# A greedy instruction list for attention: other durations, other due times, and another order for the first two units

## The chip, the cores and the metric

The kernel runs on one core of one Trainium2 chip. The metric is the device time of one execution in microseconds (us); lower is better. Before the change it is 993.29 us, the median of three runs (992.11 to 995.47).

## The reference, cut to what matters

Three stages follow each other: attention with rotary positions, an ELU network, and a bilinear network.

```python
# attention: batch 4, heads 8, sequence 576, head size 64
q_rot, k_rot = rotate(q), rotate(k)              # x1*cos - x2*sin, x1*sin + x2*cos
scores = (1 / sqrt(64)) * q_rot @ k_rot.T
attn = exp(scores - max(scores)); attn = attn / sum(attn)
x = (attn @ v)                                   # to 2304 tokens x 512
h = x @ w_in                                     # 512 x 2048
g = where(h > 0, h, exp(min(h, 0)) - 1)
x = g @ w_out                                    # 2048 x 512
return (((x @ w1) * (x @ w2)) @ w3) @ w_out2
```

## The kernel before, in words

**Units and chunks.** Attention works on 16 units, each two heads of one batch. A unit's 576 query rows are cut in four chunks of 128 rows (c = 0 to 3, both heads) and a last one of 64 rows of each head (c = 4). For c = 0 to 3 TensorE runs three parts: `Pa` (score products of the first head's first half), `Pb` (the rest of the first head and half of the second) and `Pc` (the rest), with transposes of an earlier chunk between the products. c = 4 is `S4` (`scores_4`); its stationary operand is `diag`, a block-diagonal copy of the last 64 query columns. Between these stand, for the unit before, `T4`, `l1`, `r1`, `s0` (small transposes) and `PV` (weights times v, L583 and L589).

**What each chunk costs the other engines.** VectorE takes the negative row maximum of the scores (`most`, L465), ScalarE the exp (`expo_s`, L471). TensorE needs that exp twice: to transpose it (L416) and because the exp frees the score bank in PSUM that the next chunk writes. Evacuations of the transposes (L478 on ScalarE, L480 on VectorE) go to either engine.

**Rope.** Each unit's q (576 columns) and k (640 columns) are turned by five steps each: two products with the tables `tab` (L329), an add (L332), a copy of the high part (L81, always ScalarE) and the low part (L338). The steps other than the copy go to GpSimd or VectorE. `tab[:, 1]` is the table, `tab[:, 0]` the same times the score scale. Unit 0 is turned by `first_rope` on VectorE (L358, L362, L372) in pieces, ahead of the list; its last 320 q columns come in the list (`first`, L358 to L374). Unit 1 is turned by `part` in the list: k on GpSimd, q on VectorE. GpSimd then makes unit 0's diagonal (L85) and the scaled table (L740).

**Weights.** During attention 16 tiles of the 64-bit w_in and w_out are turned into float32 (`weight_steps`): one step on ScalarE (L123), three on VectorE (L126, L129, L132).

**The list.** Nothing of this is ordered by hand. `Plan.add` takes an operation with its engine (or a choice, "pool/dve"), its duration `busy`, its latency `late` to others, a due time and its dependencies; `Plan.order` then plays the program through and emits, engine by engine, the operation that can start first, ties (within `AHEAD`, 0.2 us on VectorE) broken by due time. `ready` (not before) is at least the due time less `HOLD_0` (12 us). For a choice, `RATHER` adds a handicap: VectorE 1.2 us for rope, ScalarE 0.3 us beside GpSimd. Operations marked `lock`, and all on GpSimd, exclude each other in the list between GpSimd and VectorE. Due times come from `nom`, a clock that starts at `AT_0` and adds `busy * UNIT / 14.7` for every TensorE part:

```python
def PE(key, busy, fn, *deps, late=0.2):
    nom[key] = clock[0]
    clock[0] += busy * UNIT / 14.7
    plan.add(key, "pe", busy, late, 0.0, fn, *deps)
```

The list fixes only the order on each engine. On the chip each engine runs its queue in order and waits by semaphores for data; GpSimd's rope steps and VectorE's weight steps share no data and so no semaphore. SP issues all loads in order. `warm_up` (L826) puts dummy products on TensorE at the beginning (30, and a few between the first chunks).

Of the kernel before, what the change touches and what calls it, by code (L numbers as in the profile page):

```python
# [12 lines left out]
ALU = mybir.AluOpType  # L13
# [14 lines left out]
UNIT = 16.0  # L28
AT_0 = 14.0
# [29 lines left out]
def kernel(  # L59
# [156 lines left out]
    class Plan:  # L216
# [10 lines left out]
        def order(self):  # L227
# [51 lines left out]
    with ExitStack() as c1:  # L279
# [328 lines left out]

        def last_t(i, name):
# [8 lines left out]
        for i in range(NU + 1):  # L618
            for c in range(5):
# [34 lines left out]
                if c == 3 and more:
                    PE(("s0", i), 0.5, lambda i=i: small_0(i), ("spread", i, 0), *last_t(i, "s0"))
                if c == 3 and j >= 0:
                    PE(("PV", j, 1, 1), 1.0, lambda j=j: weigh(j, 1, (4,)), ("evl", j, 1))
                if c == 4 and j >= 0:
                    PE(("PV", j, 1, 2), 1.1, lambda j=j: weigh(j, 1, (2, 3)))

        MX, EX = OP("dve", 0.68, 0.16), OP("act", 0.73, 0.12)
        EV = OP("dve/act", dict(dve=0.58, act=0.51), 0.18)
        SP_ = lambda key, kb, due, fn, *deps, ready=EARLY: plan.add(key, "sp", 0.5, kb / 280.0, due, fn, *deps, ready=ready)
        end = clock[0]
        for i in range(NU):
# [22 lines left out]
            OP("dve/act", dict(dve=0.75, act=0.68))(("evl", i, 1), t + 0.8, lambda e, i=i: evacuate_tails(i, 1, e), ("l1", i), ("PV", i - 1, 1, 1))  # L688
            t = nom["r1", i] + 0.5
            OP("dve/act", dict(dve=0.36, act=0.29))(("evr", i, 1), t + 1.5, lambda e, i=i: evacuate_spread(i, 1, e), ("r1", i))  # L690
            t = nom["s0", i] + 0.5
            OP("dve/act", dict(dve=0.36, act=0.29))(("evl", i, 0), t + 0.4, lambda e, i=i: evacuate_tails(i, 0, e), ("s0", i), ("PV", i - 1, 0, 1))
            OP("dve/act", dict(dve=0.34, act=0.27))(("evr", i, 0), t + 0.8, lambda e, i=i: evacuate_spread(i, 0, e), ("s0", i), ("evl", i, 0))
            for hf in range(2):
# [3 lines left out]
                OP("pool/act", (dict(pool=0.4, act=0.35), dict(pool=0.9, act=0.75))[hf])(("spread", i, hf), t - (1.2, 2.0)[hf], lambda e, i=i, hf=hf: spread(i, hf, e), ("norm", i, hf), (("s0", "r1")[hf], i - 1))  # L698
# [4 lines left out]
                OP("dve", 0.36 + 0.04 * hf)(("wd", i, hf), t + (2.4, 2.2)[hf], lambda i=i, hf=hf: weighed(i, hf), dep, ("evr", i, hf))  # L703
# [17 lines left out]
        for k_ in range(5):  # L721
            eng = ("dve", "dve", "dve", "act", "dve")[k_]
            OP(eng, (0.4, 0.4, 0.4, 0.37, 0.4)[k_], lock=eng == "dve")(
                ("low", 0, 0) if k_ == 4 else ("first", 0, k_), 17.0 + 0.5 * k_, lambda k_=k_: first_step(0, 0, 256, S, dve, k_),
                *((("first", 0, k_ - 1),) if k_ else ()), ready=16.0,
            )
        OP("pool", 1.1)(("diag", 0), 21.0, lambda: diagonal(u0), ("low", 0, 0))
        for w in (1, 0):
            eng_ = (dve, pool)[w]
            n = (S, SK)[w]  # L730
            for k_ in range(5):
                eng = "act" if k_ == 3 else ("dve", "pool")[w]
                busy = 0.63 if k_ == 3 else (0.68, 1.53)[w]
                OP(eng, busy, lock=eng == "dve")(
                    ("low", 1, w) if k_ == 4 else ("first1", w, k_), (18.0, 12.0)[w] + 1.5 * k_,
                    lambda k_=k_, w=w, n=n, eng_=eng_: first_step(1, w, 0, n, eng_, k_),
                    *((("first1", w, k_ - 1),) if k_ else ()), ready=(17.0, 11.5)[w],
                )
        OP("pool", 0.7)(("diag", 1), 26.0, lambda: diagonal(units[1]), ("low", 1, 0), ("low", 1, 1))
# [818 lines left out]
```

## Time and profile before

| | us |
|---|---|
| median of three runs | 993.29 (992.11 to 995.47) |
| the profiled execution | 992.57 |
| its span (first to last instruction) | 990.8 |
| TensorE busy in it | 959.4 (97%) |
| VectorE, ScalarE, GpSimd busy | 798.4, 656.2, 216.3 |
| attention | from the start to about 289 |

The profile is one execution, recorded by the hardware. Busy shares say how full an engine is, the idle time before an instruction stands in brackets with what ended it. GpSimd has work only in attention.

### The profile page before, as it was taken

How to read it: one execution, taken by the hardware profiler on the slowest of the kernel's cores; microseconds unless marked ns; L12 is line 12 of the kernel's file. 1: busy time of each engine (PE TensorE's matmuls, PEld its weight loads, DVE VectorE, ACT ScalarE, POOL GpSimd, SP SyncE). 2: the span in 40 equal slices, each digit the busy share in tenths (PEclk: the TensorE clock that was granted, in tenths of full speed). 3: DMA queues.
4: the chain of work that ended last, by engine and by line, in shares of the span. 5: the costliest groups of instructions: out<-in, count | busy, mean ns of one | idle time of the engine just before them, and what ended most of it. 6: DMA issues, size and time to landing. Idle time of an engine off the chain costs nothing.

```text
span 990.8 us, 17967 instructions
## 1 busy us (share of the span) xinstructions
PE 959.4 (97%) x6652; PEld 833.1 (84%) x6652; DVE 798.4 (81%) x1488; ACT 656.2 (66%) x1401; POOL 216.3 (22%) x193
## 2 busy tenths in 40 slices
PE   7899989899999999999999999999999999999998
PEld 6666666666679999989999999998899999999997
DVE  7788988889889999999989999856657676675544
ACT  3777867787768778898788877774444354444332
POOL 4887877788620000000000000000000000000000
PEclk8999999999999999999999999999999999999999
DMA  7344443433322455567664676714133242224201
GB/s 242 115 145 132 141 134 121 128 137 116 108 75 80 149 169 157 189 211 233 212 191 132 209 222 228 240 34 153 37 113 88 84 139 85 75 75 153 87 28 64
DMA packets 62535, 134.53 MB, mean 136 GB/s; under 512 B 6640, under 2 KB 15472, under 8 KB 62448
## 3 DMA queue, kind: packets, MB, share of 16 engines
q1 hardware_dynamic: 62448, 133.39, 42.0%
q8 instruction: 52, 0.85, 0.4%
q14 instruction: 35, 0.29, 0.1%
HBM read 107.68 MB, written 25.69 MB: 135 GB/s over the span
## 4 chain that ended last, share of the span: by engine, by line
PE 82%; DVE 10%; ACT 4%; issue 1%; DMA 1%; POOL 1%; SPq 0%; DVEq 0%; ACTq 0%
PE y L929 12%; PE A L1359 10%; PE o L1385 10%; PE A L886 9%; PE B L1359 7%; PE B L886 7%; PE yb L930 6%; PE s L405 6%; PE o L589 5%; PE w L1289 4%; PE ptp L416 3%; DVE nm L465 2%; ACT pr L471 2%; DVE pair L129 1%; DVE pair L126 1%
## 5 line engine op out<-in xcount | busy, mean ns | idle before, releaser
L929 PE MATMUL y<-g,wo 128*128 128x512 f32 x576 | 204.2, 392 | 0.0
L930 PE MATMUL yb<-g,wo 128*128 128x256 f32 x576 | 161.3, 280 | 0.0
L140 DVE TENSOR_TENSOR set<-set 128x512 fp32r<-128x512 f32 (+1 forms) x160 | 98.3, 620 | 41.2 <-ACT set L137 41.1
L405 PEld LDWEIGHTS s<-hl 64*128 64x128 f32 x768 | 88.6, 189 | 50.0 <-ACT pr L471 37.5
L405 PE MATMUL s<-hl 64*128 64x288 f32 x768 | 110.0, 319 | 17.4 <-ACT pr L471 15.8
L929 PEld LDWEIGHTS y<-g,wo 128*128 128x128 f32 x576 | 107.8, 187 | 20.5
L471 ACT ACTIVATE pr<-s,nm 128x576 f32<-128x576 f32 x144 | 105.5, 739 | 22.5 <-DVE nm L465 21.9
L1359 PE MATMUL A<-xc,set 128*128 128x384 f32 x576 | 116.1, 336 | 0.2
L886 PE MATMUL A<-xf,set 128*128 128x384 f32 x552 | 111.5, 337 | 0.8 <-ACT p L943 0.7
L465 DVE TENSOR_REDUCE nm<-s 128x1 f32<-128x576 f32 x144 | 102.8, 748 | 11.6 <-PE s L405 10.8
L1385 PE MATMUL o<-W,g 128*128 128x512 f32 x432 | 111.1, 393 | 0.0
L1359 PEld LDWEIGHTS A<-xc,set 128*128 128x128 f32 x576 | 102.4, 188 | 7.8 <-DVE p L1446 1.0
L930 PEld LDWEIGHTS yb<-g,wo 128*128 128x128 f32 x576 | 108.6, 189 | 0.2 <-ACT xT L939 0.2
L886 PEld LDWEIGHTS A<-xf,set 128*128 128x128 f32 x552 | 93.6, 188 | 4.5 <-ACT p L943 1.5
L81 ACT ACTIVATE g<-p 128x384 fp32r<-128x384 f32 x48 | 25.2, 526 | 107.8 <-DVE p L1446 71.5
L1385 PEld LDWEIGHTS o<-W,g 128*128 128x128 f32 x432 | 80.0, 188 | 12.7
L137 ACT ACTIVATE set<-set 128x512 fp32r<-128x512 f32 (+1 forms) x160 | 89.3, 567 | 1.9 <-DMA set<-kept 1.7
L416 PE MATMUL ptp<-idt,pr 64*128 64x64 f32 x1024 | 87.9, 228 | 0.0
L329 POOL TENSOR_TENSOR raw_qk<-raw_qk,tab 128x640 f32<-128x640 f32 (+1 forms) x56 | 85.7, 1536 | 4.1 <-DMA raw_qk<-k_ 3.7
L1359 PE MATMUL B<-xc,set 128*128 128x384 f32 x432 | 86.5, 334 | 0.0
L886 PE MATMUL B<-xf,set 128*128 128x384 f32 x420 | 84.3, 336 | 0.0
L416 PEld LDWEIGHTS ptp<-idt,pr 64*128 64x128 f32 x1024 | 78.3, 141 | 0.9 <-issue 0.9
(253 smaller groups left out, 1842.5 us busy)
## 6 DMA issues: line engine op xcount, KB each, us to landing
set<-kept SPq DMA_DIRECT2D x120, 256.0 KB, 2.8
raw<-w_ SPq DMA_DIRECT2D x32, 512.0 KB, 4.1
kept<-wr SPq DMA_DIRECT2D x40, 256.0 KB, 3.2
raw_qk<-k_ SPq DMA_DIRECT2D x15, 640.0 KB, 4.0
raw_qk<-q_ SPq DMA_DIRECT2D x15, 576.0 KB, 4.3
raw<-w_in_ SPq DMA_DIRECT2D x16, 512.0 KB, 4.5
raw<-w_out_ SPq DMA_DIRECT2D x16, 512.0 KB, 4.3
w<-kept SPq DMA_DIRECT2D x24, 256.0 KB, 3.0
```

Of the source, the lines that this page charges most:

```text
L137: act.activation(t[:, 0, :w], t[:, 1, :w].bitcast(F32), ACTF.Copy)
L140: eng.tensor_tensor(t[:, 1, :w], t[:, 1, :w].bitcast(F32), t[:, 0, :w].bitcast(F32), op=ALU.subtract)
L329: eng.tensor_tensor(r[:, z], r[:, z], tab[:, w, z, TAB[w]], op=ALU.mult)
L405: pe.matmul(S_t[i, c, e][:, n, :288], w, hl[h, b, at_:at_ + 288], start=(z == 0), stop=(z == 2))
L416: pe.transpose(pts[i, c, z][:, e, kc], pr[h, at_:at_ + P], idt[h, h])
L465: dve.tensor_reduce(nm_t[i, c, e], S_t[i, c, e][:, :, :288], axis=AX.XY, op=ALU.max, negate=True)
L471: act.activation(pr_t[i, c][:, e].rearrange("p (n i) -> p n i", n=2), S_t.pop((i, c, e))[:, :, :288], ACTF.Exp, bias=nm_t.pop((i, c, e)), ...
L886: pe.matmul(banks[b][:, :HF], set_w(n, k, a, c), x[:, e, c], start=(start and i == 0), stop=i == 5, skip_group_check=True,)
L929: pe.matmul(y_t[p, o], w_, g[:, c, :512], start=s, stop=t, skip_group_check=True)
L930: pe.matmul(yb_t[p, o // 2][:, o % 2], w_, g[:, c, 512:], start=s and o % 2 == 0, stop=t, skip_group_check=True,)
L1359: pe.matmul(ps[:, :HB], w[:, a, c * P:(c + 1) * P], x[:, c, b], start=(start and i == 0), stop=i == 5, skip_group_check=True,)
L1385: pe.matmul(outs[p, o], g[:, a, o % 3 * P:o % 3 * P + P], wW[f][:, c], start=(f == 0 and i == 0), stop=(f == NG - 1 and i == 2),)
```

## The change

It does five things. The durations in attention's list are replaced: TensorE's parts by other figures, and those of VectorE, ScalarE and GpSimd by lines in the number of columns (`V_`, `A_`, `G_`, `E_`). `UNIT` goes from 16.0 to 15.5 and `AT_0` from 14.0 to 12.0. The rule of mutual exclusion lets an operation start 0.02 us before the other engine is done. Unit 0's remaining q columns are due at 12 instead of 17, and unit 0's diagonal at 14 instead of 21. Unit 1 is turned by the same steps as the others, each free to go to GpSimd or VectorE, and they wait for unit 0's diagonal; the scaled table is made by ScalarE, in front of the list.

```diff
-UNIT = 16.0
-AT_0 = 14.0
+UNIT = 15.5
+AT_0 = 12.0
+REST = 12.0
...
-                                t = max(t, free.get("lock", t))
+                                t = max(t, free.get("lock", t) - 0.02)
...
+        V_ = lambda n, fast=False: 0.00052 * n + 0.065 if fast else 0.00104 * n + 0.068
+        A_ = lambda n, sb=True: 0.00104 * n + (0.023 if sb else -0.005)
+        G_ = lambda n, tt=True: 0.00217 * n + 0.15 if tt else 0.000845 * n + 0.155
+        E_ = lambda n: dict(dve=V_(n), act=A_(n, False))
...
-                    PE(("Pa", i, c), 0.5, lambda i=i, c=c, back=back: part_a(i, c, back), *ha, ("low", i, 0), ("low", i, 1), *ta[:2])
-                    PE(("Pb", i, c), 0.4, lambda i=i, c=c: part_b(i, c), *hb)
-                    PE(("Pc", i, c), 0.5, lambda i=i, c=c, back=back: part_c(i, c, back), *ta)
+                    PE(("Pa", i, c), 0.53, lambda i=i, c=c, back=back: part_a(i, c, back), *ha, ("low", i, 0), ("low", i, 1), *ta[:2])
+                    PE(("Pb", i, c), 0.39, lambda i=i, c=c: part_b(i, c), *hb)
+                    PE(("Pc", i, c), 0.58, lambda i=i, c=c, back=back: part_c(i, c, back), *ta)
...
```

The other TensorE parts in the same way: S4 0.85 to 0.96, T4 0.5 to 0.58, the five PV 0.95, 1.35, 1.2, 1.0, 1.1 to 1.1, 1.62, 1.23, 0.88, 1.23, l1 0.35 to 0.5, r1 0.5 to 0.55, s0 0.5 to 0.45.

```diff
-        MX, EX = OP("dve", 0.68, 0.16), OP("act", 0.73, 0.12)
-        EV = OP("dve/act", dict(dve=0.58, act=0.51), 0.18)
+        MX, EX = OP("dve", V_(576)), OP("act", 0.731, 0.134)
+        EV = OP("dve/act", E_(512))
...
-            OP(eng, (0.4, 0.4, 0.4, 0.37, 0.4)[k_], lock=eng == "dve")(
-                ("low", 0, 0) if k_ == 4 else ("first", 0, k_), 17.0 + 0.5 * k_, lambda k_=k_: first_step(0, 0, 256, S, dve, k_),
-                *((("first", 0, k_ - 1),) if k_ else ()), ready=16.0,
+            OP(eng, (V_(320), V_(320), V_(320), A_(320), V_(320))[k_], lock=eng == "dve")(
+                ("low", 0, 0) if k_ == 4 else ("first", 0, k_), REST + 0.5 * k_, lambda k_=k_: first_step(0, 0, 256, S, dve, k_),
+                *((("first", 0, k_ - 1),) if k_ else ()), ready=REST,
             )
-        OP("pool", 1.1)(("diag", 0), 21.0, lambda: diagonal(u0), ("low", 0, 0))
-        for w in (1, 0):
-            eng_ = (dve, pool)[w]
-            n = (S, SK)[w]
-            for k_ in range(5):
-                eng = "act" if k_ == 3 else ("dve", "pool")[w]
...
-        OP("pool", 0.7)(("diag", 1), 26.0, lambda: diagonal(units[1]), ("low", 1, 0), ("low", 1, 1))
-        OP("pool", 1.27)(("tab",), 22.0, lambda: pool.tensor_scalar(tab[:, 0], tab[:, 1], SCALE, 1.0, op0=ALU.mult, op1=ALU.mult),
-                         ("low", 1, 1), ("first1", 0, 2), ("low", 0, 0))
+        OP("pool", 0.53)(("diag", 0), 14.0, lambda: diagonal(u0), ("low", 0, 0))
...
-                        dep = ("rope", i, w, k_ - 1) if k_ else ("ld", i, w)
+                        dep = ("rope", i, w, k_ - 1) if k_ else ("ld", i, w) if i > 1 else ("diag", 0)
                         if k_ == 3:
-                            OP("act", 0.6)(key, t + 4.6, lambda i=i, w=w, k_=k_: rope_step(i, w, k_), dep, ("S4", i - 2))
+                            OP("act", A_((S, SK)[w]))(key, t + 4.6, lambda i=i, w=w, k_=k_: rope_step(i, w, k_), dep, ("S4", i - 2))
                         else:
-                            OP("pool/dve", dict(pool=(1.43, 1.53)[w], dve=0.72), lock=True)(key, t + (0, 1.5, 3.0, 0, 5.5)[k_], lambda e, i=i, w=w, k_=k_: rope_step(i, w, k_, e), dep, ("tab",))
+                            OP("pool/dve", dict(pool=G_((S, SK)[w]), dve=V_((S, SK)[w])), 0.09, lock=True)(key, t + (0, 1.5, 3.0, 0, 5.5)[k_], lambda e, i=i, w=w, k_=k_: rope_step(i, w, k_, e), dep)
...
-                OP(eng, (0.58, 0.68, 0.8, 0.68)[k_], lock=k_ > 0)(
+                OP(eng, (A_(512), V_(512, True), V_(512), V_(512))[k_], lock=k_ > 0)(
                     ("w", m, k_), t + 1.5 * k_, lambda key=key, k_=k_: weight_step(key, k_), ("w", m, k_ - 1) if k_ else ("raw", m),
                     ("w", m - 1, k_))
...
         first_rope(units[0])
+        act.activation(tab[:, 0], tab[:, 1], ACTF.Copy, scale=SCALE)
         pool.memset(rb[1][:, 2], 0.0)
```

The remaining durations (small evacuations, spreads, diagonals, sums, the product with the row weights) are replaced in the same manner. The list behind attention is not touched.

## Rows read from the trace of the kernel before

**Rows 1.** The page, busy us of an engine, share of the span, instructions.
```profile
PE 959.4 (97%) x6652; PEld 833.1 (84%) x6652; DVE 798.4 (81%) x1488; ACT 656.2 (66%) x1401; POOL 216.3 (22%) x193
```
**Rows 2.** Stretches: length, busy time (instructions) of each engine, granted clock, DMA share, GB/s.
```profile
17.50:21.00 3.50, 0.00 (x0) 0.00 (x0) 3.50 (x5) 0.90 (x2) 2.90 (x4) 0.51 0.12 30
...
24.40:27.80 3.40, 3.40 (x32) 3.18 (x32) 2.56 (x4) 1.55 (x4) 2.19 (x2) 0.50 0.36 140
...
282.00:990.80 708.80, 703.75 (x3855) 647.08 (x3855) 556.20 (x1055) 450.24 (x917) 0.85 (x3) 1.00 0.42 135
```
**Rows 3.** Stretches from one unit's last score block to the next; fifteen, summed.
```profile
94.42:109.70 15.28, 15.07 (x174) 10.89 (x174) 12.76 (x27) 12.55 (x31) 12.61 (x11) 1.00 0.44 144
...
177.63:196.66 19.03, 15.54 (x174) 10.95 (x174) 17.08 (x27) 13.02 (x33) 13.13 (x12) 1.00 0.47 142
...
212.13:229.21 17.08, 15.38 (x174) 10.97 (x174) 14.74 (x29) 13.69 (x34) 14.31 (x11) 1.00 0.43 151
...
sum 247.74, PE 229.74 PEld 163.49 DVE 218.00 ACT 189.91 POOL 198.16; mean PE 15.32 PEld 10.90 DVE 14.53 ACT 12.66 POOL 13.21
```
**Rows 4.** Waits between 33 and 282 us: in total, times, longest us.
```profile
PE s L405 <- ACT pr L471: 16.3, 28, 1.9
```
**Rows 5.** VectorE's groups between 33 and 282 us: busy us, mean ns.
```profile
L129 DVE SCALAR_TENSOR_TENSOR pair<-raw,pair 128x512 int32<-128x512 int32 x16 | 20.3, 1271 | 0.0
L132 DVE SCALAR_TENSOR_TENSOR pair<-raw,pair 128x512 int32<-128x512 int32 x16 | 16.9, 1059 | 0.0
L126 DVE TENSOR_SCALAR pair<-pair 128x512 int32<-128x512 int32 x15 | 14.5, 970 | 0.0
```
**Rows 6.** Timeline of all engines near 90 us: start us, us, instruction.
```profile
90.09 0.40 DVE L126 TENSOR_SCALAR pair<-pair 128x512 int32<-128x512 int32 x1
...
90.72 1.55 POOL L329 TENSOR_TENSOR raw_qk<-raw_qk,tab 128x640 f32<-128x640 f32 x1
...
90.80 2.02 DVE L129 SCALAR_TENSOR_TENSOR pair<-raw,pair 128x512 int32<-128x512 int32 x1
...
94.42 1.06 PE L405 MATMUL s<-hl,diag 128*128 128x288 f32 x6 [1.14 <-ACT pr L471]
```
**Rows 7.** Timeline of VectorE near 255 us, GpSimd without a rope step beside it.
```profile
254.77 0.68 DVE L129 SCALAR_TENSOR_TENSOR pair<-raw,pair 128x512 int32<-128x512 int32 x1
```
**Rows 8.** Timeline of all engines, 9 to 34 us.
```profile
9.13 0.82 DVE L358 TENSOR_TENSOR raw_qk<-raw_qk,tab 128x288 f32<-128x288 f32 x2
...
10.96 0.46 DVE L372 TENSOR_TENSOR hl<-raw_qk,hl 128x288 fp32r<-128x288 f32 x1 [0.51 <-ACT hl L81]
...
12.04 1.42 DVE L465 TENSOR_REDUCE nm<-s 128x1 f32<-128x576 f32 x2 [0.62 <-PE s L405]
...
12.83 0.74 ACT L471 ACTIVATE pr<-s,nm 128x576 f32<-128x576 f32 x1 [1.91 <-DVE nm L465]
...
13.38 3.09 DVE L358 TENSOR_TENSOR raw_qk<-raw_qk,tab 128x320 f32<-128x320 f32 x2
...
21.66 0.60 PE L405 MATMUL s<-hl 64*128 64x288 f32 x1 [5.53 <-ACT pr L471]
...
22.54 1.06 PE L405 MATMUL s<-hl 64*128 64x288 f32 x6
...
25.61 3.05 POOL L329 TENSOR_TENSOR raw_qk<-raw_qk,tab 128x640 f32<-128x640 f32 x2 [3.67 <-DMA raw_qk<-k_]
...
28.74 1.54 POOL L332 TENSOR_TENSOR raw_qk<-raw_qk 128x640 f32<-128x640 f32 x1
...
30.23 1.41 POOL L329 TENSOR_TENSOR raw_qk<-raw_qk,tab 128x576 f32<-128x576 f32 x1
...
32.66 0.40 PE L405 MATMUL s<-hl 64*128 64x288 f32 x1 [1.12 <-DVE hl L374]
...
32.76 0.67 POOL L85 TENSOR_SCALAR diag<-hl 64x128 fp32r<-64x128 f32 x2 [1.12 <-DVE hl L374]
...
32.87 0.65 PE L405 MATMUL s<-hl 64*128 64x288 f32 x6
...
33.52 1.56 POOL L338 TENSOR_TENSOR hl<-raw_qk,hl 128x640 fp32r<-128x640 f32 x1
```

More of the change, by code (lines that the diff above doesn't have):

```diff
@@ L648 @@
+                    PE(("PV", j, 0, 0), 1.1, lambda j=j: weigh(j, 0, (0, 1)), *(("ev" + z, j, k_) for z in "xy" for k_ in (0, 1)), ("wd", j - 1, 1), ("ldv", j))
                 if c == 1 and j >= 0:
-                    PE(("l1", j), 0.35, lambda j=j: tails_1(j), *last_t(j, "l1"))
-                    PE(("PV", j, 0, 1), 1.35, lambda j=j: weigh(j, 0, (4, 2, 3)), ("evl", j, 0))
+                    PE(("l1", j), 0.5, lambda j=j: tails_1(j), *last_t(j, "l1"))
+                    PE(("PV", j, 0, 1), 1.62, lambda j=j: weigh(j, 0, (4, 2, 3)), ("evl", j, 0))
@@ L651 @@
                 if c == 2 and j >= 0:
-                    PE(("r1", j), 0.5, lambda j=j: spread_1(j), ("spread", j, 1), *last_t(j, "r1"))
-                    PE(("PV", j, 1, 0), 1.2, lambda j=j: weigh(j, 1, (0, 1)), *(("ev" + z, j, k_) for z in "xy" for k_ in (2, 3)), ("ev4", j), ("wd", j, 0))
+                    PE(("r1", j), 0.55, lambda j=j: spread_1(j), ("spread", j, 1), *last_t(j, "r1"))
+                    PE(("PV", j, 1, 0), 1.23, lambda j=j: weigh(j, 1, (0, 1)), *(("ev" + z, j, k_) for z in "xy" for k_ in (2, 3)), ("ev4", j), ("wd", j, 0))
@@ L654 @@
                 if c == 3 and more:
-                    PE(("s0", i), 0.5, lambda i=i: small_0(i), ("spread", i, 0), *last_t(i, "s0"))
+                    PE(("s0", i), 0.45, lambda i=i: small_0(i), ("spread", i, 0), *last_t(i, "s0"))
                 if c == 3 and j >= 0:
-                    PE(("PV", j, 1, 1), 1.0, lambda j=j: weigh(j, 1, (4,)), ("evl", j, 1))
+                    PE(("PV", j, 1, 1), 0.88, lambda j=j: weigh(j, 1, (4,)), ("evl", j, 1))
                 if c == 4 and j >= 0:
-                    PE(("PV", j, 1, 2), 1.1, lambda j=j: weigh(j, 1, (2, 3)))
@@ L722 @@
             eng = ("dve", "dve", "dve", "act", "dve")[k_]
-            OP(eng, (0.4, 0.4, 0.4, 0.37, 0.4)[k_], lock=eng == "dve")(
-                ("low", 0, 0) if k_ == 4 else ("first", 0, k_), 17.0 + 0.5 * k_, lambda k_=k_: first_step(0, 0, 256, S, dve, k_),
-                *((("first", 0, k_ - 1),) if k_ else ()), ready=16.0,
-            )
-        OP("pool", 1.1)(("diag", 0), 21.0, lambda: diagonal(u0), ("low", 0, 0))
-        for w in (1, 0):
-            eng_ = (dve, pool)[w]
-            n = (S, SK)[w]
-            for k_ in range(5):
-                eng = "act" if k_ == 3 else ("dve", "pool")[w]
[L733 to L738, printed above, removed]
-        OP("pool", 0.7)(("diag", 1), 26.0, lambda: diagonal(units[1]), ("low", 1, 0), ("low", 1, 1))
-        OP("pool", 1.27)(("tab",), 22.0, lambda: pool.tensor_scalar(tab[:, 0], tab[:, 1], SCALE, 1.0, op0=ALU.mult, op1=ALU.mult),
-                         ("low", 1, 1), ("first1", 0, 2), ("low", 0, 0))
-        OP("pool", 0.3)(("two",), 24.0, lambda: pool.tensor_tensor(two, idt[:, :D], idt[:, D:], op=ALU.add))
+            OP(eng, (V_(320), V_(320), V_(320), A_(320), V_(320))[k_], lock=eng == "dve")(
+                ("low", 0, 0) if k_ == 4 else ("first", 0, k_), REST + 0.5 * k_, lambda k_=k_: first_step(0, 0, 256, S, dve, k_),
+                *((("first", 0, k_ - 1),) if k_ else ()), ready=REST,
+            )
+        OP("pool", 0.53)(("diag", 0), 14.0, lambda: diagonal(u0), ("low", 0, 0))
+        OP("pool", 0.3)(("two",), 28.0, lambda: pool.tensor_tensor(two, idt[:, :D], idt[:, D:], op=ALU.add), ("diag", 0))
         for i in range(1, NU):
-            if i > 1:
+            if i:
                 t0 = nom["Pa", i, 0]
@@ L748 @@
                     m, w_ = divmod(j - 3, 2)
-                    SP_(("ld", i, w), 590, t0 - (20.0, 28.0)[w], lambda i=i, w=w: load(units[i], w), ("low", m, 1 - w_))
+                    if i > 1:
+                        SP_(("ld", i, w), 590, t0 - (20.0, 28.0)[w], lambda i=i, w=w: load(units[i], w), ("low", m, 1 - w_))
                     t = t0 - (7.5, 14.5)[w]
@@ L752 @@
                         key = ("low", i, w) if k_ == 4 else ("rope", i, w, k_)
[L753 removed]
+                        dep = ("rope", i, w, k_ - 1) if k_ else ("ld", i, w) if i > 1 else ("diag", 0)
                         if k_ == 3:
[L755 removed]
+                            OP("act", A_((S, SK)[w]))(key, t + 4.6, lambda i=i, w=w, k_=k_: rope_step(i, w, k_), dep, ("S4", i - 2))
                         else:
[L757 to L758 removed]
+                            OP("pool/dve", dict(pool=G_((S, SK)[w]), dve=V_((S, SK)[w])), 0.09, lock=True)(key, t + (0, 1.5, 3.0, 0, 5.5)[k_], lambda e, i=i, w=w, k_=k_: rope_step(i, w, k_, e), dep)
+                OP("pool/act", dict(pool=0.53, act=0.31), 0.08)(("diag", i), t0 + 3.0, lambda e, i=i: diagonal(units[i], {"pool": pool, "act": act}[e]), ("low", i, 0), ("low", i, 1), ("S4", i - 2))
         def weight_step(key, k_):
```

21 lines of the change are left out of this document (10 added, 11 removed).

## The prediction, made before the changed kernel ran

> **What bounds the kernel now.** I read the page's busy shares first: TensorE is busy 97% of the span [rows 1], so only time in which TensorE waits can be won. The stretches say where it waits [rows 2]. From 282.0 us to the end it is busy 703.75 of 708.80 us and the diff touches nothing there, so those 709 us stay. Between 17.5 and 21.0 us it is busy 0.00 us: this is the beginning that the diff reorders. Between lies attention, and I cut it at the start of each unit's last score block, which gives fifteen unit periods [rows 3]. They add up to 247.74 us with 229.74 us of TensorE work, so the mean period is 16.52 us, the work 15.32 us, and 18.0 us are waits. The periods fall into two kinds: the best is 15.28 us, the worst 19.03 us, and seven of the fifteen are 16.6 us or longer. The waits view says for what TensorE waited: 28 times for an exp of ScalarE, 16.3 us in all [rows 4].
>
> Why is that exp late? In the seven long units VectorE is busy 14.7 to 17.1 us against 12.8 us in the best one [rows 3]. The groups of VectorE show where the excess is: the three VectorE steps of a weight tile average 0.97, 1.06 and 1.27 us [rows 5], though the first takes 0.40 us [rows 6] and the one that averages 1.27 takes 0.68 us [rows 7] when no rope step of GpSimd runs beside it; the one at 1.06 has the same form and size, so I give it 0.68 too. Over the 15 + 16 + 16 steps that is 0.57 x 15 + 0.38 x 16 + 0.59 x 16 = 24 us of blocked VectorE. One collision shows how [rows 6]: GpSimd's rope step starts at 90.72, VectorE's step 0.08 us later, and VectorE ends only at 92.82, after 2.02 us; the max, the exp and TensorE behind it are late, and TensorE idles 1.14 us before 94.42. I count 27 of these 47 steps that took 0.85 us or more.
>
> **The change, part by part.** It is one program whose order comes from a greedy list; after the first two units no work of attention changes, only who stands where and, where the list may choose, on which engine.
>
> *The list's durations.* The old list gave TensorE 13.9 us a unit (four chunks of 1.4, plus 0.85, 0.5, 0.95, 0.35, 1.35, 0.5, 1.2, 0.5, 1.0, 1.1); the new one gives 15.1 (four of 1.5, plus 0.96, 0.58, 1.1, 0.5, 1.62, 0.55, 1.23, 0.45, 0.88, 1.23). The trace has 15.32 [rows 3], so the new figure is right and the old was 9% short. The period in the due times is that sum times UNIT/14.7: 15.13 us before, 15.92 us after. UNIT falls, and yet the period grows, towards the 16.52 us of the trace. With the old list VectorE and ScalarE were lined up for a TensorE that runs ahead of the real one, so on the chip they drift against GpSimd, whose rope steps have no link to the weight steps. I expect fewer lost races. The bounds: nothing won below, and above it the whole 18.0 us. A loss is not excluded (the second rival). I take what would come if half of the seven long units became like the good ones: the seven add up to 121.9 us, 17.42 us each; the good ones are near 15.4 us; 7 x 2.0 / 2 = **7 us won**. I put it at half because the better fit speaks for winning and the missing link between GpSimd and VectorE speaks against winning all.
>
> *The first unit's remaining columns.* Before, they are two VectorE steps that start at 13.38 and take 3.09 us beside unit 1's rope on GpSimd; at the same form and 288 columns two take 0.82 us at 9.13 [rows 8], so 320 columns alone would take about 0.45 each. They now get due time 12.0 and 12.5, the first max 12.505 (12.0 + 0.105 + 0.4), so two of the five stand ahead of the first max: VectorE is free at 11.42, the max starts at about 12.3 instead of 12.04 [rows 8], the third step stands ahead of the second max, which starts near 13.45 instead of 12.7. The first exp is then about 0.3 us late, the second about 0.75. What follows is no longer blocked: the second chunk's Pb at 15.0, its max at 15.45, exp at 16.2, and the third chunk on TensorE at about 17.0 instead of 21.66, where TensorE had idled 5.53 us [rows 8].
>
> *The scaled table on ScalarE.* 1280 columns; the exp of 576 takes 0.74 us, so at most 1.64 us. ScalarE idles 1.91 us before the first exp at 12.83 [rows 8], and that exp is now later, so it costs nothing; without that cover it would delay the first exp by up to 1.64 us. What GpSimd no longer spends on it was off the path.
>
> *Unit 1 like the rest.* Its ten rope steps now wait for unit 0's diagonal. Before, k ran on GpSimd as soon as it had landed, and q on VectorE. Now the low part of q is done at about 14.7, the diagonal takes 0.67 us, so GpSimd starts at 15.4. The list gives VectorE a handicap of 1.2 us for such steps, so GpSimd takes them: two k turns 3.05, an add 1.54, ScalarE's copy beside a q turn of 1.41, the low part 1.56, a turn and an add of 1.41 each, a copy (0.74, as the exp of that width) and a low part of the turn's 1.41 [rows 8]. That is 15.4 + 3.05 + 0.1 (the gap before the add) + 1.54 + 1.41 + 1.56 + 2.82 + 0.74 + 1.41 = 28.0 us. Behind it on GpSimd wait the diagonal of unit 1 and unit 2's rope, both with time to spare; the load of unit 2's q on SP's queue waits for unit 1's k and goes out near 23, later than now, for a rope that comes after 28; the weight loads queued behind it on SP are for tiles that are due at 30 and later. If the first weight tile's steps (0.4 + 0.68 + 0.68) and a spread (up to 0.7) slip in between, it is 30.5. TensorE now resumes unit 1 at 28.0 to 30.5 instead of 32.66 [rows 8]: 2.2 to 4.7 us won; I take 3.4.
>
> *The clock.* This is what is late next. At 2.8 us a chunk (from Pb over two maxes and the second exp to the next Pb: 15.0 to 17.8) TensorE finishes unit 0 near 24 and waits for that chain about 4 us. Before, the wait of 5.53 us was followed by a granted clock of half speed (1.2 GHz) from 17.5 to 27.8 us [rows 2]; six score products took 1.06 us there and 0.65 us at 32.87 [rows 8], a factor of 1.6. If the same 10.3 us of low clock fall into unit 1, where TensorE is the bound, they cost 10.3 x (1 - 1/1.6) = 3.9 us; if the clock stays high, nothing. I take 2.0. The beginning then nets 1.4 us, with bounds of -1.7 and +4.7.
>
> The Trainium skill ("TensorE: Matmul & The Clock Gate", Part 1) says the half rate is the default and that activity releases it, so an idle stretch brings it back. By that rule alone the cost would be the full 3.9 us and the beginning would lose 0.5 us.
>
> **Sum.** The profiled execution took 992.57 us, 0.7 below the median of 993.29. 992.57 - 7 - 1.4 = 984.2; set against the median that is 984.9, and I say 985.
>
> **Rivals.** *The race stays as it is.* The list only ranks; at a step's end GpSimd starts its next rope step at once, whatever the list believed, and VectorE loses when it comes 0.08 us later [rows 6]. For it: the rope durations in the list hardly change (1.43 to 1.40, 1.53 to 1.54), and so does the rule that excludes both engines at once (0.02 us). Then attention keeps 16.5 us a unit, the beginning nets zero to 2 us: 991 to 993. Against it: the old list's TensorE was 9% short. The Trainium skill ("SBUF — State Buffer", Who interferes with whom) says the one that issues first keeps the shared port for the whole instruction and the other blocks fully; the 2.02 us row agrees, and by it no list without a semaphore is safe.
>
> *Steps without room (slower).* The old list reserved 0.68 + 0.8 + 0.68 = 2.16 us of VectorE for a weight tile, the chip took 0.97 + 1.06 + 1.27 = 3.30 [rows 5], the new list reserves 0.33 + 0.60 + 0.60 = 1.53. Each max or evacuation that was planned behind a tile is then planned 0.63 us too early, 16 times: 10 us of VectorE without room. Waits of 18.0 us stand beside a shortfall of 16 x 1.14 = 18.2 today, about one for one, so up to 10 us are lost; half of it, with the other durations better, gives 998. It decides if more than 27 of the 47 steps take 0.85 us or more and the mean period passes 16.8 us.
>
> *Nearly all waits go.* Every unit at 15.4 us, as several are now: 15 x 1.1 = 17 us, with the beginning 975.
>
> *The start alone goes wrong,* with the low clock through unit 0 and unit 1 and no gain behind it: 996. It needs the rope chain past 30.5.
>
> **How the numbers follow.** Forecast 985 (979 to 990), chance 0.54; nearly all waits gone 0.12; race as before 0.18; steps without room 0.13; start alone wrong 0.03. A measurement of this kernel tells about 0.3% (3 us) from no change. Faster 0.54 + 0.12 = 0.66, same 0.18, slower 0.16. The range takes in the case of all waits gone at 975 and reaches into the slower one as far as 997, so that about 0.2 is left out; the likeliest case alone spans 979 to 990.
>
> **What would show it.** The third chunk's scores near 17 us and not 21.7; unit 1's products released near 28 to 30 by a GpSimd or VectorE low part; the granted clock between 24 and 38 us; the mean of fifteen periods near 16.0 us; the three weight steps' means under 0.9 us, with fewer than 15 of 47 over 0.85. The forecast is wrong if the period stays at 16.5 or more, or if those means don't fall.

## The result: 984.54 us, and the profile after

The changed kernel takes 984.54 us (median of four runs, 983.12 to 985.30) against 993.54 us; the ratio is 0.9907, 95% interval 0.9886 to 0.9927. That is 9.0 us faster; 985 was predicted. The size was right. Of the two reasons given for it, one does not hold, as the experiments show: the larger share does not come from fewer lost races between GpSimd and VectorE.

The page of the changed kernel, span and busy shares, answers to [rows 1]:

```profile
span 982.4 us, 17951 instructions
...
PE 959.7 (98%) x6652; PEld 833.0 (85%) x6652; DVE 795.1 (81%) x1499; ACT 650.4 (66%) x1393; POOL 218.6 (22%) x190
```

TensorE's work is what it was; 8.4 us of its waiting are gone from the span. To see where, I cut attention as before, at each unit's last score block. The stretches of the changed kernel, first unit 1, then a good unit (the best, unit 3, takes 15.19 us) and the worst, then units 2 to 15 in one (columns as in [rows 2]):

```profile
26.69:44.31 17.62, 15.67 (x169) 11.17 (x167) 14.81 (x26) 13.05 (x31) 15.50 (x14) 0.90 0.42 149
...
188.49:203.81 15.32, 15.14 (x175) 10.90 (x173) 14.04 (x28) 11.92 (x30) 14.52 (x14) 1.00 0.41 142
203.81:222.12 18.31, 15.88 (x173) 10.99 (x173) 17.30 (x29) 12.22 (x32) 13.60 (x11) 1.00 0.45 149
44.31:269.83 225.52, 215.55 (x2422) 153.18 (x2423) 206.93 (x385) 171.65 (x414) 187.54 (x153) 1.00 0.42 138
```

The kernel before, unit 1 and then units 2 to 15 in one, which [rows 3] did not hold:

```profile
30.04:46.13 16.09, 14.18 (x168) 10.52 (x167) 12.46 (x25) 12.01 (x30) 14.50 (x14) 1.00 0.47 153
46.13:277.78 231.65, 215.57 (x2422) 152.97 (x2422) 205.54 (x370) 177.90 (x423) 183.66 (x154) 1.00 0.40 128
```

So the 8.4 us of the span are 3.35 (unit 0's last block starts at 26.69, not 30.04), less 1.53 (unit 1 takes 17.62, not 16.09), plus 6.13 (units 2 to 15 take 225.52, not 231.65), plus 0.45 behind attention. The beginning nets 1.8 us up to unit 1's last block, the list 6.1 us. The mean of the fifteen periods is 16.21 us (17.62 and 225.52 together), against 16.52 before and "near 16.0" expected; of units 2 to 15, four instead of seven take 16.6 us or longer.

What TensorE waits for has not changed in kind: it still waits for exps. Waits from 30 to 274 us, against 16.3 us in [rows 4]:

```profile
PE s L406 <- ACT pr L472: 10.0, 18, 1.6
```

And the three steps of a weight tile, VectorE's groups in the same stretch, against [rows 5]:

```profile
L133 DVE SCALAR_TENSOR_TENSOR pair<-raw,pair 128x512 int32<-128x512 int32 x16 | 17.8, 1112 | 0.0
L130 DVE SCALAR_TENSOR_TENSOR pair<-raw,pair 128x512 int32<-128x512 int32 x16 | 14.9, 930 | 0.0
L127 DVE TENSOR_SCALAR pair<-pair 128x512 int32<-128x512 int32 x16 | 14.0, 873 | 0.0
```

Two of the three means fell, one rose: L126 from 0.97 to 0.87 us, L129 from 1.27 to 0.93, L132 from 1.06 to 1.11 (the lines are numbered one higher now). Under 0.9 was expected of each, and 22 of the 48 still take 0.85 us or more, where fewer than 15 were expected. By the prediction's own working, 0.47 x 16 + 0.25 x 16 + 0.43 x 16, VectorE is still blocked for about 18.5 us, against 24. So fewer races are lost, but much less changed than was forecast; what that is worth to TensorE only a test without these steps can tell.

The beginning, the timeline of all engines from 10 to 31 us, against [rows 8]:

```profile
10.91 1.26 ACT L835 ACTIVATE tab<-tab 128x1280 f32<-128x1280 f32 x1
...
11.42 0.89 DVE L359 TENSOR_TENSOR raw_qk<-raw_qk,tab 128x320 f32<-128x320 f32 x2
...
13.17 0.76 DVE L466 TENSOR_REDUCE nm<-s 128x1 f32<-128x576 f32 x1 [0.87 <-PE s L406]
...
13.97 0.74 ACT L472 ACTIVATE pr<-s,nm 128x576 f32<-128x576 f32 x1 [1.79 <-DVE nm L466]
...
15.76 0.65 POOL L86 TENSOR_SCALAR diag<-hl 64x128 fp32r<-64x128 f32 x2 [13.57 <-DVE hl L375]
...
18.18 0.40 PE L406 MATMUL s<-hl 64*128 64x288 f32 x1 [0.55 <-ACT pr L472]
...
28.36 1.43 POOL L339 TENSOR_TENSOR hl<-raw_qk,hl 128x576 fp32r<-128x576 f32 x1
...
29.84 0.39 PE L406 MATMUL s<-hl 64*128 64x288 f32 x1 [1.63 <-POOL hl L339]
```

VectorE's two steps on the remaining q columns take 0.89 us instead of 3.09, the third chunk starts at 18.18 instead of 21.66, and unit 1's products are released at 29.84 by GpSimd's low part instead of at 32.66. The granted clock of the changed kernel around that point:

```profile
27.80:31.20 3.40, 1.77 (x29) 1.51 (x30) 2.35 (x4) 2.00 (x7) 3.40 (x3) 0.96 0.33 122
31.20:34.60 3.40, 3.40 (x22) 1.93 (x24) 3.40 (x6) 2.58 (x7) 3.08 (x3) 0.53 0.50 189
34.60:38.00 3.40, 3.40 (x46) 2.47 (x45) 3.39 (x7) 3.09 (x7) 2.86 (x3) 1.00 0.00 0
```

Half speed (1.2 GHz) lasts about 3.4 us here, not the 10 us of [rows 2].

### The profile page after: what moved, and what is told of

It reads as the page before. It is cut to its first block, busy times and chain, and to the rows that moved or that the text cites. A ratio compares the mean times of both kernels' runs of the same rounds, so it can differ in the third digit from the quotient of the medians.

```text
span 982.4 us, 17951 instructions
## 1 busy us (share of the span) xinstructions
PE 959.7 (98%) x6652; PEld 833.0 (85%) x6652; DVE 795.1 (81%) x1499; ACT 650.4 (66%) x1393; POOL 218.6 (22%) x190
## 4 chain that ended last, share of the span: by engine, by line
PE 71%; DVE 3%; ACT 1%; DMA 1%; issue 1%; ACTq 0%; DVEq 0%
PE y L923 12%; PE A L1353 10%; PE o L1379 10%; PE A L880 9%; PE B L1353 7%; PE B L880 7%; PE yb L924 6%; PE w L1283 4%; PE o L590 2%; PE s L406 2%; DMA set<-kept 1%; PE ptp L417 1%; DVE set L141 0%; DVE xc L78 0%; ACT pr L472 0%
## 5 line engine op out<-in xcount | busy, mean ns | idle before, releaser
L330 POOL TENSOR_TENSOR raw_qk<-raw_qk,tab 128x640 f32<-128x640 f32 (+1 forms) x60 | 90.7, 1523 | 3.2 <-DMA raw_qk<-q_ 2.9
```

The lines of the kernel that those rows point to most:

```text
L330: eng.tensor_tensor(r[:, z], r[:, z], tab[:, w, z, TAB[w]], op=ALU.mult)
```

## The experiments

In what follows "u1" is the time of unit 1's last score block in the profiled execution and "u2-15" the fourteen periods behind it. Before: u1 46.13, u2-15 231.65. After: 44.31 and 225.52.

**1. The list alone (list_only).** The changed kernel with the old beginning; all figures of the list, UNIT 15.5 and the 0.02 us rule stay.

```diff
-AT_0 = 12.0
+AT_0 = 14.0
...
-                ("low", 0, 0) if k_ == 4 else ("first", 0, k_), REST + 0.5 * k_, lambda k_=k_: first_step(0, 0, 256, S, dve, k_),
+                ("low", 0, 0) if k_ == 4 else ("first", 0, k_), 17.0 + 0.5 * k_, lambda k_=k_: first_step(0, 0, 256, S, dve, k_),
...
-        act.activation(tab[:, 0], tab[:, 1], ACTF.Copy, scale=SCALE)
```

(and unit 1's steps, the diagonal and the table as they were before)

> The new durations, UNIT and the 0.02 us rule with the old beginning. My theory, by the stretches of the two traces (beginning 3.4 us won and 1.5 us given back in unit 1, 6.1 us won in units 2 to 15): 986.5 to 988.5, the fourteen periods after unit 1 adding up to about 226 us. Rival, the gain hangs on the beginning (the list only differs because it starts earlier): 991 to 994. Rival, the order is chaotic and any new list moves the time by a few us either way: anything from 982 to 994.

Measured: 984.67 us (981.99 to 989.82), ratio 0.9912 (0.9893 to 0.9930); u2-15 223.51. The profiled execution was the 989.82 one, with u1 at 51.83 after 20 us of half clock in its beginning; the other three runs lie between 982 and 985.3. So the list alone wins 8.1 us behind unit 1, without the new beginning. The rival that hangs the gain on the beginning falls. My own forecast for this run, 986.5 to 988.5 us, was too high.

**2. The beginning alone (begin_only).** The new beginning and AT_0 on the kernel before, every old duration. (The small `two` is due at 24, as in the kernel before.)

```diff
-AT_0 = 14.0
+AT_0 = 12.0
+REST = 12.0
...
-                        dep = ("rope", i, w, k_ - 1) if k_ else ("ld", i, w)
+                        dep = ("rope", i, w, k_ - 1) if k_ else ("ld", i, w) if i > 1 else ("diag", 0)
...
+        act.activation(tab[:, 0], tab[:, 1], ACTF.Copy, scale=SCALE)
```

> The new beginning and AT_0 with all the old durations and the old UNIT. My theory: the last block of unit 0 starts near 26.7 us as in the changed kernel, unit 1 gives back about 1.5 us for the low clock and the wait for the low part of q, units 2 to 15 stay at about 231 to 232 us: 991 to 992.5. Rival, the beginning carries the whole gain: 984 to 987. Rival, chaotic order: units 2 to 15 move by several us although nothing in their numbers changed.

Measured: 988.32 us (987.70 to 988.80), ratio 0.9957 (0.9942 to 0.9972); u1 43.40, u2-15 229.88. It wins 2.7 us to unit 1's last block and 1.8 us behind it, although no figure behind it changed. That is more than expected, and the two experiments' medians together win more (8.0 + 4.4 us against the kernel before, run beside them) than the whole change (9.0): the parts don't add up. A list whose figures behind unit 1 stay the same can still move by a couple of microseconds when its beginning changes.

**3 and 4. Which figures? (pe_old, rest_old).** First TensorE's old durations in the changed kernel, with UNIT raised so that the due times keep their period; then TensorE's new ones with all old durations of the other engines.

```diff
-UNIT = 15.5
+UNIT = 16.84
...
-                    PE(("Pa", i, c), 0.53, lambda i=i, c=c, back=back: part_a(i, c, back), *ha, ("low", i, 0), ("low", i, 1), *ta[:2])
+                    PE(("Pa", i, c), 0.5, lambda i=i, c=c, back=back: part_a(i, c, back), *ha, ("low", i, 0), ("low", i, 1), *ta[:2])
```

> The changed kernel with TensorE's old durations (13.9 us a unit) and UNIT 16.84, so that the due times keep their period of 15.92 us. My theory, that TensorE's 9% was what drifted: most of the 6 us in units 2 to 15 is lost, 989 to 991. Rival, the durations of VectorE, ScalarE and GpSimd made the gain: 984 to 985.5. Rival, chaotic order: anything from 981 to 992.

Measured: 985.39 us (983.78 to 985.48), ratio 0.9924 (0.9909 to 0.9939); u2-15 227.99. My step, that TensorE's 9% was what drifted, asked for 989 to 991 us and fails as a whole: units 2 to 15 give back 2.5 of the 6.1 us at most.

```diff
-        MX, EX = OP("dve", V_(576)), OP("act", 0.731, 0.134)
-        EV = OP("dve/act", E_(512))
+        MX, EX = OP("dve", 0.68, 0.16), OP("act", 0.73, 0.12)
+        EV = OP("dve/act", dict(dve=0.58, act=0.51), 0.18)
```

> The changed kernel with TensorE's new durations, UNIT 15.5 and the 0.02 us rule, but all old durations of VectorE, ScalarE and GpSimd. TensorE's old durations alone cost 2.5 of the 6.1 us in units 2 to 15. If the rest comes from the other engines' durations, units 2 to 15 take about 229 us here, 987 to 989. If TensorE's figures and the due times are enough, they take 226, 984 to 985.5. If the order is chaotic, no sum of parts holds and anything from 222 to 231 can come.

Measured: 989.44 us (988.56 to 990.13), ratio 0.9957 (0.9941 to 0.9974); u2-15 228.23, and u1 at 49.05 after 17 us of half clock. With the other engines' old figures 2.7 us are given back. Each half was tried in one list only, and lists with the new figures alone differ by more than that (experiments 7 to 9), so how the gain divides between the two kinds of figures is not shown.

**5 and 6. Without the weight steps (a_now, b_now).** The same edit in the changed kernel and in the kernel before. It leaves out VectorE's three steps of the 16 tiles in attention; tiles behind attention keep theirs.

```diff
-            steps_w[key][k_]()
+            if k_ == 0:
+                steps_w[key][k_]()
```

> The changed kernel without the three VectorE steps of the 16 weight tiles of attention and of all later ones made by the same function in attention's list (left out: the tiles keep what ScalarE's step wrote, so the output is not the reference's). The list still reserves their place. Theory that the lost races with GpSimd make the waits: units 2 to 15 at 213 to 216 us, nearly no wait of TensorE, and equal to the next kernel's within 1.5 us. Rival, that the new list places the maxes and evacuations better whatever the weights do: 4 us or more shorter than the next kernel's.

> The kernel before without the same VectorE steps (the same part is left out). Theory of the lost races: units 2 to 15 at 213 to 217 us, the waits of 15.9 us there fall under 4 us. Rival, better placing by the new list: units 2 to 15 at 219 us or more, 4 us or more above the kernel above.

Measured: 974.69 us (ratio 0.9810, 0.9795 to 0.9824) and 981.88 us (0.9883, 0.9868 to 0.9898). Units 2 to 15, first the changed kernel without the steps, then the kernel before without them:

```profile
45.17:261.58 216.41, 214.16 (x2422) 153.08 (x2422) 171.04 (x341) 171.08 (x414) 176.90 (x153) 1.00 0.43 144
```

```profile
45.50:267.20 221.70, 214.69 (x2422) 152.93 (x2423) 161.83 (x326) 177.47 (x423) 175.14 (x154) 1.00 0.41 138
```

The weight steps cost 231.65 - 221.70 = 9.95 us with the old list and 225.52 - 216.41 = 9.11 us with the new one: the steps, their lost races and their own time together, were and are the cause of the larger part of TensorE's waits, and the new list takes 0.8 us off that. Without any weight step the new list is still 5.3 us shorter, of 6.1 in all. So most of the gain lies in how it places the maxes, exps and evacuations; fewer lost races are not needed for it. The test takes the races and the steps' own VectorE time away at once, so it does not price the races by themselves. What stands behind the 5.3 us shows in one more pair of views, waits in the same two stretches, first the changed kernel:

```profile
PEld s L406 <- ACT pr L472: 21.3, 50, 0.8
```

```profile
PEld s L405 <- ACT pr L471: 27.5, 59, 1.1
```

TensorE's weight loads wait 6 us less for exps, and ScalarE is 6 us less busy (171.08 against 177.47), as 55 of the 112 evacuations of 512 columns go to it where the old list gave it 70. But the split alone is not the cause: the kernel with TensorE's old durations gave ScalarE less still (busy 164.64 us there) and took 227.99 us. Which placement is worth how much stays open.

**7 to 9. Is it fit or luck? (neutral, w_old, w_real).** Three small changes of figures in the changed kernel.

```diff
-        V_ = lambda n, fast=False: 0.00052 * n + 0.065 if fast else 0.00104 * n + 0.068
+        V_ = lambda n, fast=False: 0.00052 * n + 0.065 if fast else 0.00104 * n + 0.072
```

> The changed kernel with one number moved by nothing that matters: every VectorE duration 0.004 us longer (0.072 for 0.068). If the order follows from the figures' fit, units 2 to 15 stay within 1 us of 225.5 and the time within 983.5 to 985.5. If the list is chaotic, so that any other order moves the time, units 2 to 15 move by 2 us or more.

Measured: 985.51 us (982.73 to 986.18), ratio 0.9915 (0.9897 to 0.9933); u2-15 226.28, within the 1 us.

```diff
-                OP(eng, (A_(512), V_(512, True), V_(512), V_(512))[k_], lock=k_ > 0)(
+                OP(eng, (0.58, 0.68, 0.8, 0.68)[k_], lock=k_ > 0)(
```

> The changed kernel with the old reservation for a weight tile (0.58 on ScalarE; 0.68, 0.8, 0.68 on VectorE). My theory: the reservation hardly matters, 984 to 986. Rival, steps without room cost time in the changed kernel: 980 to 982.5, with fewer than 22 of the 48 steps over 0.85 us. Rival, chaotic order: 981 to 990 with no relation to the room.

Measured: 983.37 us (977.66 to 984.37), ratio 0.9896 (0.9866 to 0.9926); u2-15 222.59, with 20 of 48 steps at 0.85 us or more. That lies between my range and the rival's.

```diff
-                OP(eng, (A_(512), V_(512, True), V_(512), V_(512))[k_], lock=k_ > 0)(
+                OP(eng, (0.58, 0.94, 1.27, 1.06)[k_], lock=k_ > 0)(
```

> The changed kernel with a weight tile's steps reserved as long as the chip took for them in the kernel before (0.94, 1.27, 1.06 us on VectorE). Reserved at 0.33, 0.60, 0.60 units 2 to 15 took 225.5 us (226.3 with every VectorE figure 0.004 us longer), at 0.68, 0.8, 0.68 they took 222.6. Theory that room for the tiles lowers the waits: 220 to 223 us and 980 to 983.5. Rival, that 222.6 was the scatter of any two orders: 224 to 227 us, 984 to 986; or longer than 227, if room too wide pushes the maxes back.

Measured: 985.98 us (985.70 to 986.73), ratio 0.9933 (0.9917 to 0.9950); u2-15 227.40, with 25 steps over 0.85 us. More room for a tile first shortens attention by 3 us and then lengthens it by 2: no trend. The slower rival (steps without room) finds no support.

But the scatter has a sign. The three weight steps' busy time in units 2 to 15 orders the six lists with the new figures almost as their length does: 37.8 us in experiment 11 (221.63), 41.4 in 1 (223.51), 41.5 in 8 (222.59), 42.6 in the changed kernel (225.52), 47.3 in 7 (226.28), 47.4 in 9 (227.40). Between old and new figures it does not: experiment 10, on the old ones, has 40.8 us (with one step missing from the record) and takes 230.25. VectorE's groups in units 2 to 15, first experiment 10, then 7:

```profile
L132 DVE SCALAR_TENSOR_TENSOR pair<-raw,pair 128x512 int32<-128x512 int32 x15 | 15.5, 1033 | 0.0
L129 DVE SCALAR_TENSOR_TENSOR pair<-raw,pair 128x512 int32<-128x512 int32 x14 | 13.5, 963 | 0.0
L126 DVE TENSOR_SCALAR pair<-pair 128x512 int32<-128x512 int32 x15 | 11.8, 785 | 0.0
...
L130 DVE SCALAR_TENSOR_TENSOR pair<-raw,pair 128x512 int32<-128x512 int32 x15 | 18.2, 1212 | 0.0
L133 DVE SCALAR_TENSOR_TENSOR pair<-raw,pair 128x512 int32<-128x512 int32 x15 | 15.6, 1038 | 0.1
L127 DVE TENSOR_SCALAR pair<-pair 128x512 int32<-128x512 int32 x15 | 13.5, 901 | 0.0
```

So lost races go with the differences among lists of one kind, and not with the step from the old figures to the new.

**10. GpSimd out of the way, unit 1's q still on VectorE (first_only).** On the kernel before:

```diff
-                ("low", 0, 0) if k_ == 4 else ("first", 0, k_), 17.0 + 0.5 * k_, lambda k_=k_: first_step(0, 0, 256, S, dve, k_),
-                *((("first", 0, k_ - 1),) if k_ else ()), ready=16.0,
+                ("low", 0, 0) if k_ == 4 else ("first", 0, k_), 12.0 + 0.5 * k_, lambda k_=k_: first_step(0, 0, 256, S, dve, k_),
+                *((("first", 0, k_ - 1),) if k_ else ()), ready=12.0,
...
-                    *((("first1", w, k_ - 1),) if k_ else ()), ready=(17.0, 11.5)[w],
+                    *((("first1", w, k_ - 1),) if k_ else (("diag", 0),) if w else ()), ready=(17.0, 11.5)[w],
```

> The kernel before with only the order of GpSimd's and VectorE's first steps changed: unit 0's remaining columns due at 12, unit 1's k on GpSimd behind unit 0's diagonal; q of unit 1 stays on VectorE, the table on GpSimd, AT_0 and all durations as before. Theory that the beginning was held up by VectorE's two steps beside GpSimd's k rope: the third chunk's scores start near 18 instead of 21.7 us, the last block of unit 0 near 25 to 27, and 2 to 3 us are won up to the last block of unit 1: 990 to 991.5. Rival, that unit 1's free choice of engine (or the table) matters: no earlier than 45.5 us at the last block of unit 1, 992 to 994.

Measured: 992.55 us (990.87 to 993.59), ratio 0.9998 (0.9988 to 1.0009). Its timeline (all engines, 17 to 33 us):

```profile
17.49 2.06 DVE L358 TENSOR_TENSOR raw_qk<-raw_qk,tab 128x576 f32<-128x576 f32 x1
17.83 0.40 PE L405 MATMUL s<-hl 64*128 64x288 f32 x1 [0.55 <-ACT pr L471]
...
31.72 0.72 DVE L374 SCALAR_TENSOR_TENSOR hl<-raw_qk,hl 128x576 fp32r<-128x576 f32 x1
...
32.49 0.60 PE L405 MATMUL s<-hl 64*128 64x288 f32 x1 [1.05 <-DVE hl L374]
```

The rival held. The third chunk does start at 17.83, so the blocked VectorE steps were what held up unit 0. But unit 1's q now stands in VectorE's queue beside GpSimd's k (2.06 us for one turn) and behind maxes; its low part comes at 31.72 and TensorE resumes at 32.49, where it resumed before at 32.66. The win in unit 0 is waited away, and a half clock from 28.7 to 38.9 us makes unit 1 longer still (u1 48.37). With unit 1's q on VectorE the win does not last.

**11 and 12. TensorE kept busy ahead of unit 1 (a_warm, a_warm0).** Dummy products in place of the wait; the first time with 0.1 us in the list, the second with 0.0.

```diff
-                    PE(("warm", c), 0.1, lambda c=c: warm_up(FILL[c]))
+                    PE(("warm", c), 0.1, lambda c=c: warm_up(8 if c == 4 else FILL[c], c == 4))
+                if (i, c) == (1, 0):
+                    PE(("warm", 5), 0.1, lambda: warm_up(12, True))
...
-            ps = ps_t.tile([P, 512], F32, tag="t", name="warm") if n else None
+            ps = (ps_o.tile([P, 512], F32, tag="o", name="warm") if free else ps_t.tile([P, 512], F32, tag="t", name="warm")) if n else None
```

> The changed kernel with TensorE kept busy while it waits for unit 1's rope: 8 dummy products ahead of unit 0's last block and 12 ahead of unit 1, both in the bank that unit 0's output takes later, so they wait for no evacuation. Theory that the low clock after the wait costs 1 to 2 us in unit 1: no half clock before 40 us, unit 1's period 16 to 16.5 instead of 17.6 us, 982.5 to 983.5, with less scatter between runs. Rival, that unit 1 is late by the wait for the rope chain alone: the period stays over 17.2 us and the time at 984 to 985.5, or later by the dummies.

Measured: 980.40 us (979.30 to 981.14), ratio 0.9875 (0.9861 to 0.9890): the best of all that do the whole computation, 4.1 us under the changed kernel and below both ranges. But unit 1 takes 17.66 us, as in the changed kernel (17.62), though no half clock shows, as the rival had it; u1 is 44.13 against 44.31. The 4 us come later:

```profile
44.13:265.76 221.63, 214.70 (x2422) 153.03 (x2423) 204.10 (x391) 172.05 (x415) 185.31 (x146) 1.00 0.42 141
```

Periods agree with the changed kernel's within 0.2 us up to unit 8, then unit 9 is 1.1 us and unit 12 2.6 us shorter. Unit 12 in the changed kernel, timeline of VectorE, GpSimd and TensorE:

```profile
204.07 1.55 POOL L330 TENSOR_TENSOR raw_qk<-raw_qk,tab 128x640 f32<-128x640 f32 x1
204.14 2.03 DVE L130 SCALAR_TENSOR_TENSOR pair<-raw,pair 128x512 int32<-128x512 int32 x1
...
206.09 0.74 DVE L466 TENSOR_REDUCE nm<-s 128x1 f32<-128x576 f32 x1
...
207.75 0.66 PE L406 MATMUL s<-hl 64*128 64x288 f32 x5 [0.93 <-ACT pr L472]
```

and the same place in the kernel with the dummies:

```profile
201.35 1.54 POOL L330 TENSOR_TENSOR raw_qk<-raw_qk,tab 128x640 f32<-128x640 f32 x1
...
202.68 0.50 DVE L127 TENSOR_SCALAR pair<-pair 128x512 int32<-128x512 int32 x1
203.21 0.69 DVE L130 SCALAR_TENSOR_TENSOR pair<-raw,pair 128x512 int32<-128x512 int32 x1
203.82 0.75 DVE L466 TENSOR_REDUCE nm<-s 128x1 f32<-128x576 f32 x1
204.31 2.94 POOL L339 TENSOR_TENSOR hl<-raw_qk,hl 128x640 fp32r<-128x640 f32 x2 [1.42 <-ACT hl L82]
...
205.58 0.66 PE L406 MATMUL s<-hl 64*128 64x288 f32 x5 [0.22 <-ACT pr L472]
```

Here two weight steps run almost wholly where GpSimd waits, between 202.89 and 204.31, and take 0.50 and 0.69 us; there the step came 0.07 us behind GpSimd's and took 2.03. The 0.1 us that the dummies take in the list had shifted the due times and with them VectorE's order in places.

> The kernel with the dummies again, but they take no time in the list (0.0 for 0.1 us), so that the order on VectorE, ScalarE, GpSimd and SP is the changed kernel's line for line, and only TensorE's dummies differ. The kernel with 0.1 us took 980.4 us; its list differs from the changed kernel's in some forty lines of VectorE's 1349, and its periods are shorter in units 9 (1.1 us) and 12 (2.6 us), far from the dummies. Theory that the list's small order made those 4 us, and the clock next to nothing: units 2 to 15 at 224 to 227 us, 983.5 to 985.5. Rival, that the dummies and the clock made them: 980 to 981.5 again.

Measured: 983.80 us (982.77 to 985.47), ratio 0.9902 (0.9882 to 0.9922), no different from the changed kernel. Its units 2 to 15:

```profile
44.75:270.18 225.43, 215.42 (x2422) 153.08 (x2423) 206.73 (x386) 171.66 (x414) 187.58 (x153) 1.00 0.42 139
```

The same list gives 225.43 against 225.52 us, with unit 12 at 18.36 against 18.31: given the order, the chip repeats attention almost exactly, and in these two runs who wins a race is fixed by the list. The dummies themselves are worth next to nothing. In experiment 11 they end at 30.12, TensorE resumes unit 1 there (29.84 without them), and u1 comes 0.2 us earlier; here unit 0's last block starts only at 28.04, with a granted clock of 0.60 from 24.4 to 27.8, the dummies end at 31.7, and u1 comes 0.4 us later.

## Why the prediction was right, and where it was not

**The bound.** Right: everything behind attention took 712.57 against 713.02 us from unit 15's last block on, and the gain lies in TensorE's waits.

**The list's term, 7 us; measured 6.1.** The size holds, the reason doesn't. The step that failed reads "I expect fewer lost races", as the ground for the 7 us. VectorE's blocked time did fall, from 24 to some 18.5 us, but without the steps that lose the races the two lists still differ by 5.3 us (experiments 5 and 6), and what those steps cost TensorE fell by 0.8 us only. In its place the runs show a better placement of the ordinary work, by the new figures as a whole; which figure and which placement carry it stays open. That seven long units became four, near the half that was taken, is luck: the halving was a guess, and it met the size by another road. Six lists with the new figures (those of experiments 1, 7 to 9 and 11 and the change itself) took 221.6 to 227.4 us in units 2 to 15, three with the old ones (230.25 in experiment 10) 229.9 to 231.7, and two half-and-half ones 228.0 and 228.2: the figures together move the level by some 6 us, and the order that falls out of them scatters by some 3 us either way. So a list with nearly the same figures could have given 3 us more or less than the 6.1.

**The race rival.** Its statement that a list can't stop a race is half right. The weight steps, races and own time together, still cost 9.1 us; but the list's order decides which races are lost (experiments 11 and 12). It also said that attention would then keep 16.5 us a unit, and that doesn't follow. The Trainium skill ("SBUF — State Buffer", Who interferes with whom) says that the second of the two to issue blocks fully until the first is done. The rows at 204 us agree: GpSimd's step ends at 205.62, VectorE's, started 0.07 us after it, at 206.17, some 0.55 us later, when the same step without GpSimd beside it took 0.69 us at 203.21.

So the case "race as before", with its chance of 0.18 and its 991 to 993 us, was two statements tied together: what the weight steps cost did stay nearly as before, and the time was 984.5 us.

**The first columns.** Right in kind: two steps stand ahead of the first max and run unblocked in 0.89 us. The max came at 13.17, not 12.3, since it waited for TensorE (0.87 us in its row), which was still at its opening dummy products until 10.86, against 9.36 before. TensorE's first score products start anywhere from 9.3 to 10.8 us over the profiled runs, so this may be scatter. The third chunk came at 18.18, not 17.0.

**The table.** Right: 1.26 us from 10.91 on, and the first exp still waited 1.79 us for its max.

**Unit 1.** Right: 29.84 in a range of 28.0 to 30.5, released by GpSimd's low part; 2.8 us won, 3.4 taken. That the win does not last with unit 1's q on VectorE, experiment 10 shows.

**The clock.** Taken at 2.0 us with 3.9 at most, for 10.3 us of half clock; the profiled run shows 3.4 us of it. From TensorE's resumption of unit 1 to that unit's last block, the kernel before, the changed one, experiment 11 and experiment 10:

```profile
32.66:46.13 13.47, 12.68 (x152) 9.32 (x153) 11.04 (x23) 10.51 (x28) 12.89 (x12) 1.00 0.57 182
29.84:44.31 14.47, 14.15 (x153) 9.97 (x153) 13.82 (x24) 11.53 (x28) 12.35 (x11) 0.88 0.37 126
30.12:44.13 14.01, 13.47 (x160) 9.62 (x159) 12.67 (x23) 11.28 (x28) 12.61 (x11) 1.00 0.36 129
32.49:48.37 15.88, 15.50 (x153) 11.34 (x153) 11.44 (x22) 9.34 (x23) 8.20 (x7) 0.80 0.33 114
```

Experiment 11 starts the stretch 0.3 us later than the changed kernel, at full clock throughout, and needs 0.5 us less; so the 3.4 us of half clock cost about 0.5 us here, where the factor of 1.6 gives 1.3. Experiment 10, with 6.4 us of it behind its resumption, needs 2.4 us more than the kernel before, as much as the factor gives, though its list differs at the beginning. The other 0.5 us by which the changed kernel's stretch is longer than the one before is there at full clock too, and its cause stays open. The beginning's net was 1.8 us, 1.4 predicted: 2.8 won less 1.0, of which the clock is about half.

**The range.** The forecast's range is 979 to 990 us. The prediction's sentence that it also takes in 975 and reaches to 997 does not go with it.

## What to carry to other kernels

When a list planner's figures are brought nearer to the trace, expect the ordinary work to gain, and test a suspected contention by leaving the contending work out in both versions: those two runs tell how much of the gain is there without it, though not what the contention costs apart from the work's own time. An order from a greedy list repeated on the chip to 0.2 us a period here but jumps by microseconds with a 0.1 us change of one figure, so a single variant says little of its edit; compare several lists of each kind, or hold the order fixed, as the last experiment does. Where two versions of a list differ only by such luck, a few can simply be tried: one of them is 4 us faster here, and the weight steps' busy time shows why.

## What was not expected

The same list (the changed kernel and experiment 12) repeats each of its periods behind unit 1 within 0.2 us, lost races included, in kernels whose unit 1 ends half a microsecond apart. The beginning is what scatters between runs: the profiled executions spent between nothing (experiment 11) and 20 us of it at half clock (experiment 1, whose profiled run took 989.82 us where its others took 982 to 985.3). UNIT with the old period and the 0.02 us rule were not tried singly.
